# Shuffle reads issued later, more staging buffers, and another layout for the first batch, in a Fourier filter followed by a swish MLP

## The chip, the cores and the metric

The kernel runs on one core of one Trainium2 chip. The metric is the device time of one execution in microseconds (us). Most executions of one kernel agree within 0.3 to 0.5% in one round.

The engines are TensorE (PE; its weight loads are listed apart as PEld), VectorE (DVE), ScalarE (ACT), GpSimd (POOL) and SyncE (SP). SyncE does no arithmetic: it issues DMA transfers, in program order, and waits in that order too.

## The reference

A global filter along the sequence (rfft, product with a learned filter, irfft), then an MLP with the activation h * sigmoid(beta * h). Cut to what matters:

```python
# x: (8, 3008, 256); filt_r, filt_i: (1505, 256)
X = np.fft.rfft(x, axis=1)
y = np.fft.irfft(X * (filt_r + 1j * filt_i)[None], n=3008, axis=1)
# w_in: (256, 2048), w_out: (2048, 256), beta: (2048,)
h = y.reshape(8 * 3008, 256) @ w_in
out = (h / (1 + np.exp(-beta * h))) @ w_out
```

## The kernel before

The Fourier transform of length 3008 = 47 x 64 is done as two stages of matmuls with tables (stage 1 and stage 2), the product with the filter, and two inverse stages (3 and 4). Between the stages the data must change its place in the partitions.

For batch 0 this happens inside the core, in a **prologue**, with transposes on TensorE. For batches 1 to 7 it goes through DRAM. Each shuffle is a write of staging tiles and a read in another order: stage 1 writes d1, and a2 is read from it; stage 3 writes d2, and zz is read from it; stage 4 writes dy, and y is read from it by a transposing DMA.

The MLP is the **main loop** of 752 steps. A step handles 512 tokens and 128 hidden units: two matmuls into `hps`, a Silu on ScalarE into `gT`, and, two steps later, four matmuls into `acc`. Every 16 steps finish a block of 512 tokens. The filter work of the next batch is mixed in between the steps. A **window** is the stretch of steps that consume one batch: w0 has 80 steps, w1 to w7 have 96 each. In window w the stages 2 to 4 of batch w+1 and stage 1 of batch w+2 are placed; w0 also holds stage 1 of batch 1.

```python
apool = pool("apool", 3)          # staging tiles of stages 1 and 4, one tag
...
# prologue, batch 0: the inverse output of stage 3, one eviction per two frequencies
z_t = ypool.tile([P, NDC, J, KP], BF16, name="z_t", tag="y")      # J = 32, KP = 96
...
            evac(
                z_t[:, :, :, 4 * k0 : 4 * k0 + 8].rearrange("p c j a -> p c a j"),
                ps.rearrange("p c e (a j) -> p c (e a) j", j=J),
                True,                                              # on ScalarE
            )
...
def turn(g):                       # transposes: z_t is the stationary operand
    ...
                    nc.tensor.transpose(
                        pz[:KP, e, dc * P : (dc + 1) * P],
                        z_t[:, dc, JG * g + 4 * i + e, :],
                        ident[:],
                    )
...
def s1(b, i, on_act):              # a unit of stage 1, 16 units per batch
    ...
        s["a1"] = apool.tile([KP, JG, D], BF16, name="a1", tag="a1")   # each 4 units
    ...
    evac(s["a1"][:, jj : jj + 2, :], ps[:KP], on_act)
    if jj + 2 == JG:
        nc.sync.dma_start(s["d1r"][:, g * JG : (g + 1) * JG, :], s["a1"][:])
        if g == J // JG - 1:       # reads at once behind the last write
            ...
                nc.sync.dma_start(t[:], s["d1c"][:, h * KG : (h + 1) * KG, :])   # a2
            if b + 1 < B:
                xs[b + 1] = load_x(b + 1)
...
def place(w, lo, hi, units, clear=False):      # one unit per step at most
    a, z = first_step[w], first_step[w + 1]
    for n, go in enumerate(units):
        at = a + (z - a) * (lo + (hi - lo) * n / max(1, len(units) - 1))
        at = min(int(at), z - 1)
        if clear and (at % NFB < 2 or at % NFB > 13):
            at += (2 - at) % NFB
        while at in plan:
            at += 1
        plan[at] = go
...
    if w_ == 0:
        place(w_, 0.00, 0.15, u1(b, 0, n1, True))     # stage 1 of batch 1
        place(w_, 0.29, 0.62, u23(b), True)           # stages 2 and 3
        place(w_, 0.76, 0.87, u4(b))                  # stage 4
        if b + 1 < B:
            place(w_, 0.63, 0.75, u1(b + 1, 0, n1))   # stage 1 of the next batch
    else:
        place(w_, 0.03, 0.48, u23(b), True)
        place(w_, 0.64, 0.79, u4(b))
        if b + 1 < B:
            place(w_, 0.49, 0.63, u1(b + 1, 0, n1))
```

In `place`, stage 1 of the next batch comes last and moves past any taken step. Its 16 units do not fit in front of stage 4. In w0 the last eight of them (four of these only in w1), and in w1 to w5 the last three, therefore run behind stage 4.

## Time and profile before

The median was 901.64 us (901.03 to 905.14, four runs). The profiled execution took 894.5 us, which is at the fast end.

The page of the profile, first: busy time by engine, rows of busy tenths in 40 equal slices of the span of 892.4 us (PEclk is the granted TensorE clock in tenths), and two groups of instructions (line, engine, operation, shapes, count | busy us, mean ns | idle before).

```profile
PE 799.7 (90%) x5634; PEld 551.4 (62%) x5723; DVE 425.0 (48%) x656; ACT 617.0 (69%) x893; POOL 175.3 (20%) x189
...
PE   7449899559989999799978999799999999999997
...
PEclk9759999879989999999998999899999999999999
...
L662 ACT ACTIVATE gT<-hps,beta_sb 128x512 bf16<-128x512 f32 x752 | 516.5, 687 | 248.2 <-PE hps L653 226.9
...
L99 ACT ACTIVATE z_t<-psz 128x512 bf16<-128x512 f32 x12 | 31.2, 3023 | 4.6 <-PE psz L387 4.5
```

TensorE is busy 90% of the span. The clock row has holes: each digit below 9 is a slice in which TensorE ran partly at half speed. The two groups show the same shape, 128x512 float32 to bfloat16 on ScalarE. It takes 687 ns where the output is contiguous (gT) and 3023 ns where it is scattered (z_t).

The table of stretches (us from the span's start; busy us and count per engine; clock; DMA share; GB/s). The first two rows are the z_t evictions and the "turning" that follows them, up to the first Silu. The other rows are w0, w1 and w2.

```profile
core 0: us, PE busy (x) PEld busy (x) DVE busy (x) ACT busy (x) POOL busy (x), PEclk, DMA share, GB/s
31.60:65.80 34.20, 17.16 (x119) 11.81 (x119) 13.67 (x27) 34.10 (x14) 14.91 (x16) 0.60 0.43 76
65.80:77.10 11.30, 9.56 (x131) 8.32 (x132) 7.14 (x12) 5.36 (x14) 11.01 (x13) 0.87 0.32 94
77.10:179.60 102.50, 85.90 (x556) 56.87 (x566) 54.34 (x80) 64.07 (x101) 22.59 (x27) 0.94 0.61 151
179.60:296.50 116.90, 103.66 (x684) 69.11 (x694) 56.72 (x84) 71.56 (x108) 20.41 (x22) 0.92 0.49 124
296.50:400.40 103.90, 97.39 (x680) 67.27 (x689) 54.02 (x80) 71.70 (x108) 19.39 (x20) 0.98 0.52 139
```

In the first row ScalarE is busy 34.1 of 34.2 us: it is the limit there. In the other rows, compare the length with TensorE's busy time: 102.5 against 85.9 in w0, 117 against 103.7 in w1. The clock column is below 1.00 in all of them, so part of that busy time is itself stretched.

The waits (engine, line, what it waited for: us in total, times, longest):

```profile
PE hps L653 <- DMA y<-dy: 9.9, 2, 7.7
...
PE ps_2124 L516 <- DMA a_2093<-d_1676: 8.5, 1, 8.5
...
DVE a_2897 L101 <- DMA d_2716<-a_2719: 6.7, 1, 6.7
...
PE ps_2935 L567 <- DVE a_2897 L101: 4.1, 1, 4.1
```

And the chain of waits in w2 (start, duration, what), which shows how two of those lines hang together:

```profile
249.54 0.44 PE acc L680 x4
249.98 0.43 PE hps L653 x2
250.83 9.34 DMA d_2716<-a_2719
260.26 0.70 DVE a_2897 L101
...
261.59 0.85 PE acc L680 x4
```

The chain leaves TensorE at 250.4 us for the shuffle write of the oldest staging tile, which takes until 260.2 us. A stage-1 eviction (`a_2897`) needs a tile, all three are in use, and so it stands 6.7 us. TensorE itself works on until 256.9 us and then stands 4.1 us, because its next matmul waits for that eviction. From 261.0 us it goes on, at first with four acc matmuls in 0.85 us where they took 0.44 us before: half clock.

A last reading is worked out from the starts of the 752 Silu evictions in the trace. In w7, without filter work, eight steps take 7.0 us: that is the floor of TensorE.

| | first Silu at | w0 | w1 | w2 | w3 | w4 | w5 | w6 | w7 |
|---|---|---|---|---|---|---|---|---|---|
| before (us) | 77.1 | 102.5 | 117.0 | 103.9 | 105.3 | 104.9 | 99.8 | 92.5 | 83.0 |

### The profile page before, as it was taken

What the parts mean: (1) busy time and instruction counts of PE and PEld (TensorE: products, weight loads), DVE (VectorE), ACT (ScalarE), POOL (GpSimd) and SP (SyncE); (2) the same over time, 40 slices, a digit from 0 to 9 for tenths busy, and PEclk for the clock granted to TensorE, in tenths of its full rate; (3) what the DMA queues carried; (4) which work ended last, traced back from release to release, by engine and by line L of the source; (5) the groups of instructions that cost most, each with busy time, mean ns of one, the idle gap of its engine ahead of it and who ended that gap; (6) DMA issues with size and microseconds to landing.
All of it is one profiled execution on the core that took longest, in us unless ns stands there. A gap on an engine that the chain in (4) does not pass through costs nothing.

```text
span 892.4 us, 14629 instructions
## 1 busy us (share of the span) xinstructions
PE 799.7 (90%) x5634; PEld 551.4 (62%) x5723; DVE 425.0 (48%) x656; ACT 617.0 (69%) x893; POOL 175.3 (20%) x189
## 2 busy tenths in 40 slices
PE   7449899559989999799978999799999999999997
PEld 4336566337646776467655776467765676667665
DVE  7725485336544475427546265353656365421101
ACT  5797676328746787478854787467875788777775
POOL 4825251013200232003310132101310032000000
PEclk9759999879989999999998999899999999999999
DMA  8815627751186524674174821857135721551011
GB/s 168 170 38 112 171 77 208 159 145 60 55 222 134 166 86 110 182 169 132 59 176 136 210 73 47 217 120 192 60 96 188 198 67 61 171 129 48 24 49 48
DMA packets 132281, 110.06 MB, mean 123 GB/s; under 512 B 47010, under 2 KB 117683, under 8 KB 132211
## 3 DMA queue, kind: packets, MB, share of 16 engines
q1 hardware_dynamic: 127570, 95.74, 38.5%
q0 software_dynamic: 4640, 13.37, 8.9%
q8 instruction: 45, 0.74, 0.3%
q14 instruction: 26, 0.20, 0.1%
HBM read 54.01 MB, written 57.67 MB: 125 GB/s over the span
## 4 chain that ended last, share of the span: by engine, by line
PE 73%; DMA 12%; DVE 2%; issue 2%; SPq 2%; ACT 1%; POOL 0%; DVEq 0%; POOLq 0%; ACTq 0%
PE acc L680 33%; PE hps L653 30%; SPq L584 2%; DMA d_6478<-a_6481 1%; DMA d_3970<-a_3973 1%; DMA d_1676<-a_1679 1%; DMA d_5224<-a_5227 1%; DMA d_2716<-a_2719 1%; DMA y<-dy 1%; DMA d_7732<-a_7813 1%; DVE ost L692 1%; DVE yo L103 1%; DMA d_933<-a_1080 1%; DMA d_1676<-a_2040 1%; DMA d_5224<-a_5405 0%
## 5 line engine op out<-in xcount | busy, mean ns | idle before, releaser
L662 ACT ACTIVATE gT<-hps,beta_sb 128x512 bf16<-128x512 f32 x752 | 516.5, 687 | 248.2 <-PE hps L653 226.9
L680 PE MATMUL acc<-wout_sb,gT 128*128 128x256 bf16 x3008 | 461.1, 275 | 4.8 <-DVE ost L692 1.3
L653 PE MATMUL hps<-y,win_sb 128*128 128x512 bf16 (+7 forms) x1643 | 435.6, 354 | 10.2 <-DMA y<-dy 9.9
L680 PEld LDWEIGHTS <-gT 128*128 128x128 bf16 x3008 | 295.7, 99 | 187.7 <-issue 33.1
L653 PEld LDWEIGHTS <-win_sb 128*128 128x128 bf16 x1728 | 166.7, 99 | 34.9 <-issue 10.0
L534 POOL TENSOR_TENSOR v_t<-p_t,q_t 128x512 bf16<-128x512 f32 x84 | 106.5, 1268 | 305.9 <-DVE q_t L528 245.1
L692 DVE COPY ost<-acc 128x512 f32<-128x512 f32 x94 | 60.4, 684 | 200.8 <-PE acc L680 200.8
L113 POOL DMA_DIRECT2D xg<-in_x_dram x32 | 17.5, 546 | 238.2 <-PE ps_5651 L494 30.0
L516 PEld LDWEIGHTS <-t_102 128*128 128x128 bf16 x168 | 16.1, 98 | 29.7 <-issue 15.2
L99 ACT ACTIVATE z_t<-psz 128x512 bf16<-128x512 f32 x12 | 31.2, 3023 | 4.6 <-PE psz L387 4.5
L387 PE MATMUL psz<-t_103,pb_t 128*128 128x128 bf16 x48 | 10.1, 281 | 17.3 <-ACT z_t L99 10.7
L567 PEld LDWEIGHTS <-t_101 96*96 96x96 bf16 x112 | 14.3, 128 | 15.7 <-issue 2.1
L494 PEld LDWEIGHTS <-t_100 94*96 94x96 bf16 x112 | 13.9, 124 | 15.5 <-issue 2.8
L544 PEld LDWEIGHTS <-t_103 128*128 128x128 bf16 x168 | 16.0, 98 | 7.6 <-issue 2.3
L149 POOL TENSOR_SCALAR wout_sb<-ws,rbeta_sb 128x256 bf16<-128x256 f32 x16 | 14.5, 937 | 19.6 <-issue 19.3
L114 POOL DMA_DIRECT2D xg<-in_x_dram x32 | 16.4, 514 | 0.0
L184 PE MATMUL pw<-wz 128*128 128x512 bf16 x37 | 14.2, 470 | 1.2 <-DVE wz L178 1.2
L387 PEld LDWEIGHTS <-qb_t 128*128 128x128 bf16 x48 | 6.1, 129 | 11.6 <-issue 6.2
L138 POOL TENSOR_SCALAR fi_sb<-fi_sb 64x1536 f32<-64x1536 f32 x3 | 12.9, 4330 | 0.1
L387 PEld LDWEIGHTS <-pb_t 128*128 128x128 bf16 x48 | 6.3, 132 | 9.6 <-DVE pb_t L377 9.2
L387 PE MATMUL psz<-t3q,qb_t 128*128 128x128 bf16 x48 | 10.1, 286 | 0.5 <-DVE qb_t L378 0.5
L427 PE MATMUL pz<-ident,z_t 128*96 128x128 bf16 x64 | 5.4, 258 | 4.8 <-ACT z_t L99 4.8
(1037 smaller groups left out, 659.3 us busy)
## 6 DMA issues: line engine op xcount, KB each, us to landing
out_dram<-ost SPq DMA_DIRECT2D x47, 512.0 KB, 3.0
dy<-yo SPq DMA_DIRECT2D x28, 384.0 KB, 3.0
xg<-in_x_dram POOLq DMA_DIRECT2D x32, 320.0 KB, 6.0
ws<-in_moe_w_out_dram SPq DMA_DIRECT2D x4, 512.0 KB, 6.2
xg<-in_x_dram POOLq DMA_DIRECT2D x32, 56.0 KB, 6.0
fr_sb<-in_filt_r_dram SPq DMA_DIRECT2D x8, 192.0 KB, 6.3
fi_sb<-in_filt_i_dram SPq DMA_DIRECT2D x8, 192.0 KB, 7.2
d_934<-z SPq DMA_DIRECT2D x4, 384.0 KB, 2.8
```

The lines of the kernel that those rows point to most:

```text
L99: nc.scalar.activation(dst, src, ACT.Copy, scale=1.0 if scale is None else scale)
L113: nc.gpsimd.dma_start(t[:80], xv[:80, js, :])
L114: nc.gpsimd.dma_start(t[80:NP], xv[80:NP, js, :])
L387: nc.tensor.matmul(ps[:, dc, e, :], lhsT=src[:, e, dc * P : (dc + 1) * P], rhs=tab[:, k0 + e, :, :].rearrange("p c k -> p (c k)"), start=f ...
L516: nc.tensor.matmul(ps[:, e, :], lhsT=t2[:, k0 + e, :, :].rearrange("p c k -> p (c k)"), rhs=s["a2"][g][:, kk + e, :], start=True, stop=True,)
L534: nc.gpsimd.tensor_tensor(v_t[:], p_t[:], q_t[:], ALU.add)
L544: nc.tensor.matmul(ps[:, e, :], lhsT=t3[:, k0 + e, :, :].rearrange("p c k -> p (c k)"), rhs=v_t[:, e, :], start=True, stop=True,)
L584: nc.sync.dma_start_transpose(ys[b][:, c, :S], s["dy"][c, :S, :])
L653: nc.tensor.matmul(hps[:, pos - t0 : pos - t0 + ln], lhsT=win_sb[:, dc, fb * P : (fb + 1) * P], rhs=ys[b][:, dc, n0 : n0 + ln], start=(dc ...
L662: nc.scalar.activation(gT[:, :tn], hps[:, :tn], ACT.Silu, scale=beta_sb[:, fb : fb + 1])
L680: nc.tensor.matmul(acc[tb // 2][:, tb % 2, :], lhsT=gT[:, tb * P : (tb + 1) * P], rhs=wout_sb[:, fb, :], start=(fb == 0 and tb % 2 == 0), ...
L692: nc.vector.tensor_copy(ost[:, 2 * h : 2 * h + n, :], acc[h][:, :n, :])
```

## The change

Its intent: (a) issue the shuffle reads some steps after their writes, so that SyncE's in-order queue is not held up by them; (b) six staging tiles instead of three; (c) place stage 1 of the next batch ahead of stage 4, with two units per step in w0, every second one evicted by ScalarE; (d) in the prologue write z_t contiguously; (e) share the prologue's table work out differently: table evictions and fewer multiplies, the negated copies of the imaginary filter all on GpSimd, the beta constants computed earlier.

```diff
-    apool = pool("apool", 3)
+    apool = pool("apool", 6)
...
-            lo = AP(filt.tensor, filt.offset + k0 * D, [[N1 * D, H], [D, KG], [1, D]])
+            lo = AP(filt.tensor, filt.offset + k0 * D, [[N1 * D, H], [1, KG * D]])
...
+        ks_ = slice(8 * i, 8 * i + 8)
+        evac(t3[:, ks_, :, :].rearrange("p k c m -> p k (c m)"), pt[:], False)
+        for lo, to in ((M, 0), (0, M)):
+            evac(t3q[to : to + M, ks_, :, :]..., pt[lo : lo + M], True)
...
-    nc.vector.tensor_scalar_mul(fi_sb[:M, 0, :], fi_sb[:M, 0, :], keep[:M])
-    copy_imag(0, nc.vector)
-    copy_real(0)
-    nc.vector.tensor_scalar_mul(t3q[:, :, 0, :], t3[:, :, 1, :], nsg[:])
-    nc.vector.tensor_scalar_mul(t3q[:, :, 1, :], t3[:, :, 0, :], sg[:])
-    for g in range(1, NK // KG):
+    nc.gpsimd.tensor_scalar_mul(fi_sb[:M, 0, :], fi_sb[:M, 0, :], keep[:M])
+    for g in range(NK // KG):
         copy_imag(g, nc.gpsimd)
...
-    z_t = ypool.tile([P, NDC, J, KP], BF16, name="z_t", tag="y")
+    z_t = ypool.tile([P, NDC, KP, J], BF16, name="z_t", tag="y")
...
-                z_t[:, :, :, 4 * k0 : 4 * k0 + 8].rearrange("p c j a -> p c a j"),
-                ps.rearrange("p c e (a j) -> p c (e a) j", j=J),
+                z_t[:, :, 4 * k0 : 4 * k0 + 8, :].rearrange("p c (e a) j -> p c e (a j)", e=2),
+                ps[:],
...
-                        z_t[:, dc, JG * g + 4 * i + e, :],
+                        z_t[:, dc, :, JG * g + 4 * i + e],
...
     (the reads of a2, zz and y move out of s1, s23 and s4 into a2_read, zz_read, y_read)
...
         if w_ == 0:
-            place(w_, 0.00, 0.15, u1(b, 0, n1, True))
-            place(w_, 0.29, 0.62, u23(b), True)
-            place(w_, 0.76, 0.87, u4(b))
+            place(w_, 0.00, 0.14, u1(b, True))
+            place(w_, 0.19, 0.19, [lambda b=b: a2_read(b)], per=9)
+            place(w_, 0.28, 0.60, u23(b), True)
+            place(w_, 0.645, 0.645, [lambda b=b: zz_read(b)], per=9)
             if b + 1 < B:
-                place(w_, 0.63, 0.75, u1(b + 1, 0, n1))
+                place(w_, 0.61, 0.71, u1(b + 1, True), per=2)
+                place(w_, 0.78, 0.78, [lambda b=b: a2_read(b + 1)], per=9)
+            place(w_, 0.72, 0.81, u4(b, True), per=2)
+            place(w_, 0.85, 0.85, [lambda b=b: y_read(b)], per=9)
         else:
             place(w_, 0.03, 0.48, u23(b), True)
+            place(w_, 0.525, 0.525, [lambda b=b: zz_read(b)], per=9)
+            if b + 1 < B:
+                place(w_, 0.49, 0.63, u1(b + 1))
+                place(w_, 0.71, 0.71, [lambda b=b: a2_read(b + 1)], per=9)
             place(w_, 0.64, 0.79, u4(b))
-            if b + 1 < B:
-                place(w_, 0.49, 0.63, u1(b + 1, 0, n1))
+            place(w_, 0.84, 0.84, [lambda b=b: y_read(b)], per=9)
```

More of the change, by code (lines that the diff above doesn't have):

```diff
@@ L128, in load_filters @@
             )
-            nc.sync.dma_start(f_sb[:H, k0 : k0 + KG, :], lo)
+            nc.sync.dma_start(f_sb[:H, k0 : k0 + KG, :].rearrange("p k d -> p (k d)"), lo)
             nc.sync.dma_start(f_sb[H:M, k0 : k0 + KG, :], hi)
@@ L225 @@
     )
-    ip_f = small("ip_f")
-    nc.vector.tensor_copy(ip_f[:], ip[:])
-    nc.vector.tensor_scalar(ident[:], ic[:], ip_f[:], None, ALU.is_equal)
     m_p = bits("m_p", ip[:], ALU.bitwise_and, M - 1)
@@ L252 @@
     )
+    nc.vector.tensor_scalar(r[:], u[:], ROUND_C, ROUND_C, ALU.add, ALU.subtract)
+    nc.vector.tensor_tensor(u[:], u[:], r[:], ALU.subtract)
     def t2_part(part):
         if part == 0:
-            nc.vector.tensor_scalar(r[:], u[:], ROUND_C, ROUND_C, ALU.add, ALU.subtract)
+            nc.scalar.activation(t2[:, :, 0, :], u[:], ACT.Sin, scale=TWO_PI)
         elif part == 1:
-            nc.vector.tensor_tensor(u[:], u[:], r[:], ALU.subtract)
-            nc.scalar.activation(t2[:, :, 0, :], u[:], ACT.Sin, scale=TWO_PI)
-        elif part == 2:
             nc.scalar.activation(r[:], u[:], ACT.Abs)
@@ L270 @@
     gp = nc.gpsimd
-    hs, k2, keep, keep2, sg, nsg = (
-        small(n) for n in ("hs", "k2", "keep", "keep2", "sg", "nsg")
-    )
+    ip_f = small("ip_f")
+    gp.tensor_copy(ip_f[:], ip[:])
+    gp.tensor_scalar(ident[:], ic[:], ip_f[:], None, ALU.is_equal)
+    hs, k2, keep, keep2 = (small(n) for n in ("hs", "k2", "keep", "keep2"))
     gp.tensor_scalar(hs[:], m_p[:], float(H), None, ALU.is_ge)
@@ L281 @@
     gp.tensor_scalar(keep[:], keep[:], 1.0, None, ALU.add)
-    gp.tensor_scalar(sg[:], hs[:], -2.0, 1.0, ALU.mult, ALU.add)
-    gp.tensor_scalar(nsg[:], c_p[:], 2.0, -1.0, ALU.mult, ALU.add)
-    gp.tensor_tensor(nsg[:], nsg[:], sg[:], ALU.mult)
-    gp.tensor_scalar(sg[:], nsg[:], -1.0, None, ALU.mult)
     nc.gpsimd.memset(t4[:], 0.0)
@@ L304 @@
                 ps[:, :, :KP].rearrange("p j k -> p k j"),
-                dc == 1,
+                i < 4 or (i < 6 and dc == 1),
             )
         warm(2)
-        if i % 2 == 1:
-            t2_part(i // 2)
+        if i >= 3 and i < 6:
+            t2_part(i - 3)
     a2s = []
@@ L324 @@
                 )
-        evac(a2s[-1][:, 3 * (i % 2) : 3 * (i % 2) + 3, :], pb[:], i % 2 == 1)
+        evac(a2s[-1][:, 3 * (i % 2) : 3 * (i % 2) + 3, :], pb[:], False)
+    bps = opsum.tile([P, NFB], F32, name="bps", tag="acc")
+    id_f = setup.tile([NFB, NFB], F32, name="id_f", tag="id_f")
+    nc.vector.tensor_copy(id_f[:], ident[:NFB, :NFB])
+    nc.tensor.transpose(bps[:], bt[:], id_f[:])
+    tiny = setup.tile([P, NFB], F32, name="tiny", tag="tiny")
+    nc.vector.tensor_copy(beta_sb[:], bps[:])
+    nc.vector.tensor_tensor(tiny[:], beta_sb[:], beta_sb[:], ALU.mult)
+    nc.vector.tensor_scalar(tiny[:], tiny[:], 1e-12, None, ALU.is_lt)
+    nc.vector.scalar_tensor_tensor(beta_sb[:], tiny[:], 2e-6, beta_sb[:], ALU.mult, ALU.add)
+    nc.vector.reciprocal(rbeta_sb[:], beta_sb[:])
+    copy_real(0)
     for i in range(3):
@@ L333 @@
             )
-        evac(t3[:, 8 * i : 8 * i + 8, :, :].rearrange("p k c m -> p k (c m)"), pt[:], i != 0)
+        ks_ = slice(8 * i, 8 * i + 8)
+        evac(t3[:, ks_, :, :].rearrange("p k c m -> p k (c m)"), pt[:], False)
+        for lo, to in ((M, 0), (0, M)):
+            evac(
+                t3q[to : to + M, ks_, :, :].rearrange("p k c m -> p k (c m)"),
+                pt[lo : lo + M],
+                True,
+            )
     tp = opsum.tile([KP, NP], BF16, name="tp", tag="acc")
@@ L399 @@
         warm(1)
-    bps = opsum.tile([P, NFB], F32, name="bps", tag="acc")
-    id_f = setup.tile([NFB, NFB], F32, name="id_f", tag="id_f")
-    nc.vector.tensor_copy(id_f[:], ident[:NFB, :NFB])
-    nc.tensor.transpose(bps[:], bt[:], id_f[:])
-    tiny = setup.tile([P, NFB], F32, name="tiny", tag="tiny")
-    nc.vector.tensor_copy(beta_sb[:], bps[:])
-    nc.vector.tensor_tensor(tiny[:], beta_sb[:], beta_sb[:], ALU.mult)
-    nc.vector.tensor_scalar(tiny[:], tiny[:], 1e-12, None, ALU.is_lt)
-    nc.vector.scalar_tensor_tensor(beta_sb[:], tiny[:], 2e-6, beta_sb[:], ALU.mult, ALU.add)
-    nc.vector.reciprocal(rbeta_sb[:], beta_sb[:])
     sp.close()
@@ L499, in s1, with a2_read @@
             nc.sync.dma_start(s["d1r"][:, g * JG : (g + 1) * JG, :], s["a1"][:])
-            if g == J // JG - 1:
-                s["a2"] = []
-                for h in range(NK // KG):
-                    t = a2pool.tile([P, KG, D], BF16, name="a2", tag="a2")
-                    nc.sync.dma_start(t[:], s["d1c"][:, h * KG : (h + 1) * KG, :])
-                    s["a2"].append(t)
-                if b + 1 < B:
-                    xs[b + 1] = load_x(b + 1)
+            if g == J // JG - 1 and b + 1 < B:
+                xs[b + 1] = load_x(b + 1)
+    def a2_read(b):
+        s = st[b]
+        s["a2"] = []
+        for h in range(NK // KG):
+            t = a2pool.tile([P, KG, D], BF16, name="a2", tag="a2")
+            nc.sync.dma_start(t[:], s["d1c"][:, h * KG : (h + 1) * KG, :])
+            s["a2"].append(t)
     def s23(b, i):
@@ L553, in s23, with zz_read, s4 @@
                 nc.sync.dma_start(s["d2c"][:, g * KG : (g + 1) * KG, :], s["z"][:])
-                if g == NK // KG - 1:
-                    s["zz"] = []
-                    for h in range(J // JG):
-                        t = zzpool.tile([KP, JG, D], BF16, name="zz", tag="zz")
-                        nc.sync.dma_start(t[:], s["d2r"][:, h * JG : (h + 1) * JG, :])
-                        s["zz"].append(t)
-    def s4(b, i):
+    def zz_read(b):
+        s = st[b]
+        s["zz"] = []
+        for h in range(J // JG):
+            t = zzpool.tile([KP, JG, D], BF16, name="zz", tag="zz")
+            nc.sync.dma_start(t[:], s["d2r"][:, h * JG : (h + 1) * JG, :])
+            s["zz"].append(t)
+    def s4(b, i, on_act):
         s = st[b]
@@ L572, in s4 @@
             ps[:KP].rearrange("p (j c d) -> p c j d", j=2, c=NDC),
-            False,
+            on_act,
             inv_scale,
@@ L580, in s4, with y_read @@
             )
-            if g == J // JG - 1:
-                ys[b] = ypool.tile([P, NDC, NK * P], BF16, name="y", tag="y")
-                for c in range(NDC):
-                    nc.sync.dma_start_transpose(ys[b][:, c, :S], s["dy"][c, :S, :])
-                del st[b]
+    def y_read(b):
+        s = st.pop(b)
+        ys[b] = ypool.tile([P, NDC, NK * P], BF16, name="y", tag="y")
+        for c in range(NDC):
+            nc.sync.dma_start_transpose(ys[b][:, c, :S], s["dy"][c, :S, :])
     NBLK = (TOK + TB - 1) // TB
@@ L594, with place, u1 @@
     plan = {}
-    def place(w, lo, hi, units, clear=False):
+    def place(w, lo, hi, units, clear=False, per=1):
         a, z = first_step[w], first_step[w + 1]
+        last_at = a
         for n, go in enumerate(units):
             at = a + (z - a) * (lo + (hi - lo) * n / max(1, len(units) - 1))
-            at = min(int(at), z - 1)
+            at = max(min(int(at), z - 1), last_at)
             if clear and (at % NFB < 2 or at % NFB > 13):
                 at += (2 - at) % NFB
-            while at in plan:
+            while len(plan.get(at, ())) >= per:
                 at += 1
-            plan[at] = go
-    def u1(b, lo, hi, act=False):
+            plan.setdefault(at, []).append(go)
+            last_at = at
+    def u1(b, act=False):
         def unit(i):
@@ L615, in unit, with u4 @@
             return go
-        return [unit(i) for i in range(lo, hi)]
+        return [unit(i) for i in range(J // 2)]
     def u23(b):
         return [lambda i=i: s23(b, i) for i in range(NK // 2 + VLAG)]
-    def u4(b):
-        return [lambda i=i: s4(b, i) for i in range(J // 2)]
+    def u4(b, act=False):
+        return [lambda i=i: s4(b, i, act and i % 2 == 1) for i in range(J // 2)]
     for w_ in range(B - 1):
         b = w_ + 1
-        n1 = J // 2
         if w_ == 0:
-            place(w_, 0.00, 0.15, u1(b, 0, n1, True))
-            place(w_, 0.29, 0.62, u23(b), True)
-            place(w_, 0.76, 0.87, u4(b))
+            place(w_, 0.00, 0.14, u1(b, True))
+            place(w_, 0.19, 0.19, [lambda b=b: a2_read(b)], per=9)
+            place(w_, 0.28, 0.60, u23(b), True)
+            place(w_, 0.645, 0.645, [lambda b=b: zz_read(b)], per=9)
             if b + 1 < B:
-                place(w_, 0.63, 0.75, u1(b + 1, 0, n1))
+                place(w_, 0.61, 0.71, u1(b + 1, True), per=2)
+                place(w_, 0.78, 0.78, [lambda b=b: a2_read(b + 1)], per=9)
+            place(w_, 0.72, 0.81, u4(b, True), per=2)
+            place(w_, 0.85, 0.85, [lambda b=b: y_read(b)], per=9)
         else:
             place(w_, 0.03, 0.48, u23(b), True)
+            place(w_, 0.525, 0.525, [lambda b=b: zz_read(b)], per=9)
+            if b + 1 < B:
+                place(w_, 0.49, 0.63, u1(b + 1))
+                place(w_, 0.71, 0.71, [lambda b=b: a2_read(b + 1)], per=9)
             place(w_, 0.64, 0.79, u4(b))
-            if b + 1 < B:
-                place(w_, 0.49, 0.63, u1(b + 1, 0, n1))
+            place(w_, 0.84, 0.84, [lambda b=b: y_read(b)], per=9)
     blk = {}
@@ L666 @@
         if s in plan:
-            plan[s]()
+            for go in plan[s]:
+                go()
         if s >= LAG:
```

## The prediction

> **What bounds it now** (table of stretches; starts of the 752 Silu evictions). A prologue: first Silu at 77.1 us. The main loop, 752 steps: in the last 96, free of filter work, eight steps take 7.0 us, TensorE at full clock. With a batch of filter work mixed in, 96 steps need about 96 us (92.5 were taken by window 6, which lacks only 16 stage-1 matmuls of 0.21 us). The windows took: w0 (80 steps) 102.5, w1 117.0, w2 to w4 103.9, 105.3, 104.9, w5 99.8, w6 92.5, w7 83: 16 us in w0, 21 in w1, 4 to 9 in each of w2 to w5 are TensorE stalls, some 66 us together. Then a tail of 6 us.
>
> **The stalls** (waits, chain of waits, DMA issues). In w2 to w4 a stage-1 eviction waits 7 to 10 us for the shuffle write of an earlier staging tile (three buffers; the write queues behind four zz reads and lands after 9 to 11 us instead of 3 to 6). TensorE idles 4 to 6 us in stage 4, then runs 3.4 to 6.8 us at half clock. In w0 the transposing y reads land 8 to 10 us late. In w1 the a2 reads are 8.5 us late: the last stage-1 units were pushed behind stage 4. The Trainium skill, "TensorE: Matmul & The Clock Gate", section "HAM oscillation", says that waits over about 3.4 us bring the half clock; this trace's clock agrees.
>
> **The prologue.** From 31.6 to 65.8 us ScalarE limits: twelve z_t evictions 2.6 us apart (3.02 us each, elements scattered 192 bytes apart). The same shape written contiguously took 0.69 us (gT).
>
> **What the change does.**
> - z_t: 12 x (2.6 - 0.6) = 24 us off ScalarE. GpSimd limits next, with all four negated filter copies (4.1 to 4.3 us each) after the t4 scaling: about 26 + 1.3 + 0.8 + 4 x 4.2 + 1.6 = 46 us, then three pairs of products (1.2 us each): z_t ends near 51, not 66. The turning transposes now load weights at a 64-byte stride; the skill's "SBUF — State Buffer" (cachelines note) warns of that, no trace here prices it; I allow 1 us. First Silu near 62: **-15 us**.
> - VectorE loses a 4.5 us t3q multiply, ScalarE gains six table evictions of 1 us: even.
> - Six staging buffers, stage 1 wholly before stage 4: w2 to w4 near 97 each, **-23**; w5 **-3**.
> - w1, a2 read early: near 97, **-20**.
> - w0: stage 4 ends at step 66 of 80, not 75; y follows some 14 us later, near step 80; 0 to 3 us of stall may stay: **-14**.
> - Contiguous filter loads, early beta: under 1.
>
> No matmul gets shorter. Sum -75 of 902: **827 us**, 8 in 10 within **812 to 848**. Faster by over 2%: 0.97; within 2%: 0.02; slower: 0.01.
>
> **What would show it.** First Silu at 58 to 66 us; z_t evictions near 0.7 us; late products waiting for GpSimd's fi copies; w1 to w5 at 95 to 99 us, eight steps at most 9; no half clock after 75 us except perhaps at the end of w0; no stage-1 eviction waiting on a shuffle write; matmul count unchanged, TensorE busy above 94%.
>
> **What would make it wrong.** Strided weight loads at 0.1 to 0.2 us more each (64: +6 to 13 us). The y read, issued at step 80 of 96 beside the last stage-4 unit, needing 14 us: each window boundary could stall 1 to 4 us and drop the clock. x loads, now earlier, colliding with a2 reads and yo writes. ScalarE, with doubled units in w0, delaying Silu.

## More of the kernel before

The instructions on the tile z_t (durations in ns as min/median/max, first and last start):

```profile
L427 PEld LDWEIGHTS <-z_t x64: 123/123/203, 65.9 to 73.2; 128*96 128x96 bf16 x64
...
L99 ACT ACTIVATE z_t<-psz x12: 2727/3121/3122, 31.6 to 62.7; 128x512 bf16<-128x512 f32 x12
```

## The result

The changed kernel took 845.59 us in the median (842.92 to 846.41, four runs) against 901.64. The ratio is 0.9366, 95% interval 0.9334 to 0.9398. Ratios here are the mean time of one kernel's fast runs over that of the other's of the same rounds, so they are not quite the ratios of the medians quoted. The time lies within the stated range, 19 us above the stated value.

| | first Silu at | w0 | w1 | w2 | w3 | w4 | w5 | w6 | w7 |
|---|---|---|---|---|---|---|---|---|---|
| before (us) | 77.1 | 102.5 | 117.0 | 103.9 | 105.3 | 104.9 | 99.8 | 92.5 | 83.0 |
| after (us) | 67.6 | 110.5 | 98.9 | 96.3 | 96.3 | 96.3 | 96.3 | 92.5 | 83.0 |
| difference | -9.5 | +8.0 | -18.1 | -7.6 | -9.0 | -8.6 | -3.5 | 0 | 0 |

The differences add up to -48.3 us, which is the difference of the two profiled spans (892.4 and 844.1). The medians differ by 56 us, because the profiled execution of before was 7 us faster than its median.

So w1 to w5 gained as foreseen, the prologue gained less, and w0 became longer. The page after, in the lines that answer to those of before:

```profile
PE 797.0 (94%) x5634; PEld 553.8 (66%) x5723; DVE 410.9 (49%) x638; ACT 602.0 (71%) x911; POOL 179.9 (21%) x189
...
PE   7589886979999999999999999999999999999997
...
PEclk9778998889999999999999999999999999999999
...
L674 ACT ACTIVATE gT<-hps,beta_sb 128x512 bf16<-128x512 f32 x752 | 516.1, 687 | 193.4 <-PE hps L665 171.4
...
L99 ACT ACTIVATE z_t<-psz 128x512 bf16<-128x512 f32 x12 | 7.1, 597 | 8.8 <-PE psz L395 8.7
```

TensorE is busy 94% of a span of 844.1 us. The clock row is now 9 from the tenth slice (190 us) on. The z_t evictions take 597 ns instead of 3023. The same stretches as before (z_t evictions, turning, w0, w1, w2):

```profile
32.70:49.10 16.40, 13.01 (x118) 8.86 (x118) 12.56 (x21) 9.98 (x14) 16.29 (x14) 0.88 0.56 92
49.10:67.60 18.50, 17.49 (x131) 16.21 (x132) 7.41 (x12) 5.31 (x12) 14.28 (x16) 0.63 0.51 118
67.60:178.20 110.60, 90.87 (x562) 58.76 (x571) 46.29 (x68) 72.10 (x117) 23.51 (x28) 0.92 0.66 161
178.20:277.10 98.90, 98.19 (x680) 66.90 (x690) 54.20 (x80) 71.50 (x108) 19.31 (x20) 0.97 0.52 143
277.10:373.40 96.30, 95.59 (x680) 66.70 (x689) 54.19 (x80) 71.71 (x109) 19.32 (x20) 1.00 0.53 147
```

The z_t stretch fell from 34.2 to 16.4 us, and GpSimd, busy 16.29 us of it, is now its limit. The turning grew from 11.3 to 18.5 us with the same 131 matmuls. In w2 TensorE is busy 95.6 of 96.3 us at full clock: no wait is left to be removed there. The instructions on z_t:

```profile
L424 PEld LDWEIGHTS <-z_t x64: 238/257/269, 49.1 to 62.8; 128*96 128x96 bf16 x64
...
L99 ACT ACTIVATE z_t<-psz x12: 592/597/597, 32.7 to 48.5; 128x512 bf16<-128x512 f32 x12
```

The weight loads of the turning went from a median of 123 ns to 257. The waits:

```profile
PE ps_1800 L570 <- DMA zz<-d_932: 7.7, 1, 7.7
...
DVE qb_t L386 <- POOL fi_sb L138: 6.1, 2, 5.0
...
PE hps L665 <- DMA y<-dy: 4.6, 2, 2.6
...
PE ps_1208 L517 <- DMA a_1131<-d_931: 3.8, 1, 3.8
```

The wait for a staging tile is gone. A wait of 7.7 us for zz in w0 is new. SyncE's queue in w0 (start, time, issue) shows how late zz is:

```profile
131.47 0.32 SPq L496 DMA_DIRECT2D d_1615<-a_1618  x1
132.52 0.36 SPq L554 DMA_DIRECT2D d_932<-z  x1
139.61 2.43 SPq L561 DMA_DIRECT2D zz<-d_932  x4
```

And in the kernel before:

```profile
140.33 1.73 SPq L558 DMA_DIRECT2D zz<-d_934  x4
```

The reads of zz wait 7 us for the last write of d2, which stands right behind a stage-1 write of batch 2. They are issued 72.0 us after the start of w0 (139.6 - 67.6). Before it was 63.2 us (140.3 - 77.1). Yet stage 4 was moved ahead, from step 60 to step 58, while the last unit of stage 3 stands at step 51 in both kernels.

The 8.8 us have two parts. The last write of d2 is issued 4.6 us later in the window (64.9 us after its start against 60.3), since the steps before it took longer. And it takes 7.1 us until SyncE can go on, where it took 2.9 us before. Then the first read of zz takes 8.0 us to land instead of 3.7. Beside these transfers (130 to 140 us) SyncE and GpSimd issued a stage-1 write, an output write and eight loads of x; in the kernel before there was only an output write.

### The profile page after: what moved, and what is told of

The parts are those of the page before. It is cut to its first block, busy times and chain, and to the rows that moved or that the text cites. A ratio compares the mean times of both kernels' runs of the same rounds, so it can differ in the third digit from the quotient of the medians.

```text
span 844.1 us, 14640 instructions
## 1 busy us (share of the span) xinstructions
PE 797.0 (94%) x5634; PEld 553.8 (66%) x5723; DVE 410.9 (49%) x638; ACT 602.0 (71%) x911; POOL 179.9 (21%) x189
## 2 busy tenths in 40 slices
DMA packets 132280, 110.06 MB, mean 130 GB/s; under 512 B 47009, under 2 KB 117682, under 8 KB 132210
## 4 chain that ended last, share of the span: by engine, by line
PE 85%; DMA 7%; issue 3%; DVE 2%; POOL 2%; SPq 1%; ACT 1%; DVEq 0%; POOLq 0%; ACTq 0%
PE acc L693 38%; PE hps L665 35%; DMA fi_sb<-in_filt_i_dram 2%; PE pz L424 1%; DVE ost L705 1%; POOL fi_sb L138 1%; DMA zz<-d_932 1%; DMA xg<-in_x_dram 1%; DMA dy<-yo 1%; DMA y<-dy 1%; DMA d_931<-a_1078 1%; DMA a_3015<-d_2714 1%; DMA a_6777<-d_6476 0%; DMA a_1131<-d_931 0%; DVE q_t L529 0%
## 5 line engine op out<-in xcount | busy, mean ns | idle before, releaser
L114 POOL DMA_DIRECT2D xg<-in_x_dram x32 | 16.4, 513 | 0.0
L138 POOL TENSOR_SCALAR fi_sb<-fi_sb 64x1536 f32<-64x1536 f32 x4 | 16.3, 4100 | 0.1
L395 PE MATMUL psz<-t3q,qb_t 128*128 128x128 bf16 x48 | 7.9, 244 | 8.3 <-DVE qb_t L386 7.7
L99 ACT ACTIVATE z_t<-psz 128x512 bf16<-128x512 f32 x12 | 7.1, 597 | 8.8 <-PE psz L395 8.7
L424 PE MATMUL pz<-ident,z_t 128*96 128x128 bf16 x64 | 11.2, 353 | 0.5 <-ACT z_t L99 0.5
L424 PEld LDWEIGHTS <-z_t 128*96 128x96 bf16 x64 | 10.8, 257 | 0.8 <-ACT z_t L99 0.8
L101 DVE COPY zz<-pz 96x1024 bf16<-96x1024 bf16 x8 | 5.5, 687 | 9.8 <-PE pz L424 9.8
```

Of the source, the lines that this page charges most:

```text
L114: nc.gpsimd.dma_start(t[80:NP], xv[80:NP, js, :])
L138: eng.tensor_scalar_mul(fi_sb[M:P, ks_, :], fi_sb[:M, ks_, :], -1.0)
L424: nc.tensor.transpose(pz[:KP, e, dc * P : (dc + 1) * P], z_t[:, dc, :, JG * g + 4 * i + e], ident[:],)
```

## The experiments

Twelve kernels ran; each gave correct results. Each was timed beside the kernel before on its own chip; the median of before was 898 to 902 us in the four groups (runs 1 to 4, 5 to 8, 9 and 10, 11 and 12; one chip each). Runs of different groups are best compared by their ratios. The table of windows gives the first Silu and the windows in us, worked out as above from each trace; w6 (92.5) and w7 (83.0) were the same in all.

| run | median | ratio to before | first Silu | w0 | w1 | w2 | w3 | w4 | w5 |
|---|---|---|---|---|---|---|---|---|---|
| after | 845.59 | 0.9366 | 67.6 | 110.5 | 98.9 | 96.3 | 96.3 | 96.3 | 96.3 |
| 1 z_t scattered again | 853.97 | 0.9469 | 78.5 | 107.1 | 98.8 | 96.3 | 96.3 | 96.3 | 96.2 |
| 2 z_t in runs | 834.23 | 0.9248 | 58.7 | 106.9 | 97.9 | 96.3 | 96.6 | 96.3 | 96.2 |
| 3 three buffers | 881.42 | 0.9773 | 68.2 | 114.0 | 105.2 | 103.5 | 104.6 | 105.2 | 98.2 |
| 4 first window earlier | 830.98 | 0.9219 | 67.3 | 97.2 | 97.6 | 96.3 | 96.3 | 96.3 | 96.3 |
| 5 reads at once | 842.90 | 0.9376 | 67.4 | 108.7 | 97.9 | 96.3 | 96.3 | 96.3 | 96.3 |
| 6 before, six buffers | 861.81 | 0.9579 | 77.6 | 101.3 | 111.5 | 96.5 | 98.1 | 97.0 | 97.1 |
| 7 runs 2 and 4 together | 825.44 | 0.9176 | 59.4 | 98.7 | 97.8 | 96.3 | 96.3 | 96.3 | 96.3 |
| 8 first copy on VectorE | 820.46 | 0.9125 | 54.6 | 98.6 | 97.9 | 96.3 | 96.3 | 96.3 | 96.3 |
| 9 x load later | 819.73 | 0.9103 | 54.5 | 97.8 | 97.6 | 96.3 | 96.3 | 96.3 | 96.3 |
| 10 a2 read before stage 4 | 822.30 | 0.9134 | 54.5 | 100.5 | 97.7 | 96.3 | 96.3 | 96.3 | 96.3 |
| 11 x load spread | 816.95 | 0.9049 | 54.5 | 95.0 | 97.9 | 96.3 | 96.3 | 96.3 | 96.3 |
| 12 a2 read after y | 810.74 | 0.8982 | 54.5 | 91.0 | 96.3 | 96.3 | 96.3 | 96.3 | 96.3 |

### 1. z_t scattered again

```diff
-    z_t = ypool.tile([P, NDC, KP, J], BF16, name="z_t", tag="y")
+    z_t = ypool.tile([P, NDC, J, KP], BF16, name="z_t", tag="y")
...   (eviction and transposes as in the kernel before)
```

> The changed kernel with the first batch's inverse output z_t laid out and evicted as before (single elements 192 bytes apart). Theory (the new layout trades ScalarE time for strided weight loads): z_t evictions return to about 3.0 us each and the twelve of them end 15 to 18 us later (about 65 instead of 49 us), but the turning stretch from the last of them to the first Silu shrinks from 18.5 to about 11 us, with weight loads back from 257 to about 156 ns; first Silu at 75 to 78 us, total +8 to +11 us (853 to 857). Rival (the turning stretch is long for another cause, such as GpSimd or DMA work that now falls beside it): the turning stretch stays above 15 us and the total grows by 15 us or more.

Measured: 853.97 us, 8 us more than the changed kernel. The evictions are back at 3023 ns in the mean. The last of them starts at 63.5 us, and the first Silu is at 78.5 us. The weight loads are back at a median of 140 ns, and the turning from the first transpose (66.7 us) takes 11.8 us. So the layout alone is worth about 11 us at the first Silu: 17 us gained by the evictions and 7 us given back in the turning. The rival, another cause for the long turning, falls.

### 2. z_t in runs of 16 bytes

The old layout, but the eviction follows the order of the destination. PSUM is then read with strides instead, and eight bfloat16 elements are written side by side.

```diff
-                z_t[:, :, 4 * k0 : 4 * k0 + 8, :].rearrange("p c (e a) j -> p c e (a j)", e=2),
-                ps[:],
+                z_t[:, :, :, 4 * k0 : 4 * k0 + 8],
+                ps.rearrange("p c e m -> p c (e m)").rearrange("p c (a j) -> p c j a", j=J),
...   (z_t as [P, NDC, J, KP] and the transposes as in the kernel before)
```

> The changed kernel with the old layout of z_t, but the eviction walks it in the order of the destination, so that eight elements (16 bytes) are written side by side and PSUM is read strided. Theory (scattered two-byte writes made the old eviction slow, strided weights make the new turning slow): evictions at 0.6 to 0.8 us, weight loads at about 156 ns, turning stretch about 11 us, first Silu near 60 us, total -6 to -9 us (837 to 840). Rival (strided PSUM reads cost as much as scattered writes): evictions at 1.5 us or more and no gain.

Measured: 834.23 us, better than expected. The instructions on z_t in this run, and its turning as a row of the table of stretches:

```profile
L424 PEld LDWEIGHTS <-z_t x64: 119/123/125, 48.8 to 54.8; 128*96 128x96 bf16 x64
...
L99 ACT ACTIVATE z_t<-psz x12: 591/597/598, 32.3 to 48.1; 128x512 bf16<-128x512 f32 x12
```

```profile
48.80:58.70 9.90, 8.24 (x131) 6.99 (x133) 6.96 (x12) 5.34 (x13) 7.66 (x9) 1.00 0.91 201
```

Both sides are had: evictions at 597 ns as in the contiguous layout, weight loads at 123 ns as in the old one. The turning takes 9.9 us at full clock. The scattered writes, not the layout, made the old eviction slow; strided reads of PSUM cost nothing here.

This run also prices the strided weight load. The first thirty-two transposes took 2.03 us here at full clock, 63 ns each. In the changed kernel they took 5.51 us, 172 ns each, beginning at full clock too: the clock fell only in the course of the turning, as two more rows of its table of stretches show.

```profile
49.00:53.00 4.00, 3.88 (x24) 3.88 (x24) 1.37 (x2) 0.07 (x1) 4.00 (x5) 1.00 1.07 212
53.00:57.00 4.00, 3.68 (x32) 3.55 (x31) 1.83 (x3) 1.34 (x3) 3.17 (x4) 0.59 0.82 208
```

64 x (172 - 63) ns = 7.0 us, of the 8.6 us by which the turning is longer than here (18.5 against 9.9). That it grew by nearly the same 7.0 us, namely 7.2, from before to after is luck: the kernel before began its turning at half clock too, 27 transposes 107 ns apart instead of 56, which is 1.4 us by estimate. The half clock came on top, from the second of these rows on, although TensorE is recorded as busy all the time. It cost the transposes little (sixteen took 2.83 us, 177 ns each), it may account for the other 1.6 us of the turning, which was not measured apart, and it cost 1.5 us in the first eight steps of w0 (9.5 against 8.0 us). Why the clock fell is not shown. It is not that transposes alone cannot bring the full clock: in the kernel before TensorE stood from 61.0 to 65.9 us, then ran transposes alone, and at 68.7 us these went from 107 to 56 ns apart. In the changed kernel they start 165 ns apart; that this left the array idle between them is an argument only.

### 3. Three buffers

```diff
-    apool = pool("apool", 6)
+    apool = pool("apool", 3)
```

> The changed kernel with three staging buffers instead of six. Theory (the buffers remove the mid-window stall of w2 to w5): a stage-1 eviction again waits for the shuffle write of an earlier tile, w2 to w5 go from 96.3 to 101 to 105 us each, total +20 to +40 us. Rival (placing stage 1 wholly ahead of stage 4 and the reads behind the writes removed the stall, the buffers hardly matter): w2 to w5 stay below 98 us, total within 6 us of the changed kernel.

Measured: 881.42 us, +36 us. The waits of this run:

```profile
DVE a L101 <- DMA d<-a: 37.6, 5, 8.7
...
PE ps L491 <- DVE a L101: 24.8, 6, 6.0
```

The wait of stage-1 evictions for shuffle writes is back, and TensorE's 6 us waits with it. w2 to w4 are at 103.5 to 105.2 us, as in the kernel before. The rival, that placement removed this stall, falls: without the buffers the new placement is no better in w2 to w4 than the old.

### 4. First window earlier

```diff
-            place(w_, 0.00, 0.14, u1(b, True))
-            place(w_, 0.19, 0.19, [lambda b=b: a2_read(b)], per=9)
-            place(w_, 0.28, 0.60, u23(b), True)
-            place(w_, 0.645, 0.645, [lambda b=b: zz_read(b)], per=9)
+            place(w_, 0.00, 0.09, u1(b, True), per=2)
+            place(w_, 0.12, 0.12, [lambda b=b: a2_read(b)], per=9)
+            place(w_, 0.23, 0.53, u23(b), True)
+            place(w_, 0.56, 0.56, [lambda b=b: zz_read(b)], per=9)
             if b + 1 < B:
-                place(w_, 0.61, 0.71, u1(b + 1, True), per=2)
+                place(w_, 0.57, 0.67, u1(b + 1, True), per=2)
```

> The changed kernel with the first window's stages 1 to 3 of batch 1 placed earlier (stage 1 two units per step, stages 2 and 3 over 0.23 to 0.53 of the window, zz read at 0.56, stage 1 of batch 2 at 0.57 to 0.67); stage 4 unchanged. Theory (w0 is bound by the latency of the chain of shuffles; stage 4 was placed before its zz data could land): the 7.7 us wait for zz falls below 2 us, the half-clock stretch after it goes, w0 falls from 110.5 to 93 to 98 us, total -12 to -17 us (829 to 833). Rival (w0 is bound by engines or DMA volume, doubled units crowd ScalarE and VectorE): w0 stays above 104 us.

Measured: 830.98 us, and w0 at 97.2. All that TensorE still waits for a DMA in the main loop:

```profile
PE hps L665 <- DMA y<-dy: 3.8, 2, 2.4
...
PE ps L517 <- DMA a<-d: 2.0, 1, 2.0
```

The wait for zz is gone. w0 was bound by the latency of its chain of shuffles, not by engines or by the amount of data in all: the same units, more crowded than before, fit into 13 us less. The run does two things at once, though: the front of the chain starts earlier, and the zz reads (issued at 123.8 us) now go ahead of the stage-1 writes and x loads of the next batches (from 125.5 us on). How much each gave is not shown.

### 5. Reads at once

Every read goes back behind its last write; buffers and placement stay.

```diff
+            if g == J // JG - 1:
+                a2_read(b)
+                if b + 1 < B:
+                    xs[b + 1] = load_x(b + 1)
...   (zz_read and y_read likewise; the seven placed reads are taken out)
```

> The changed kernel with every shuffle read issued directly behind its last write again, buffers and placement kept. Theory (the delay of the reads is worth little once there are six buffers and stage 1 is wholly ahead of stage 4): w2 to w5 within 1 us of 96.3 each; in w0 the a2 reads of batch 2 now go ahead of the yo writes, so y comes 2 to 5 us later; total +0 to +6 us. Rival (the delay itself removed the stalls of w2 to w5): these windows go back above 99 us each, total +12 us or more.

Measured: 842.90 us, ratio 0.9376 (0.9348 to 0.9404) against 0.9366 for the changed kernel: no difference that the runs could show. w2 to w5 are 96.3 us each. The delay of the reads, the first item of the change, is worth nothing once there are six buffers. A detail of the expectation missed: y did not come later. TensorE's wait for it fell from 4.6 to 2.4 us. In this run stage 4 itself was held 8.3 us by zz.

### 6. The kernel before with six buffers

```diff
-    apool = pool("apool", 3)
+    apool = pool("apool", 6)
```

> The kernel before with six staging buffers and nothing else changed. Theory (the buffers alone cure w2 to w4, the placement cures w1): w2 to w5 at 96 to 98 us each instead of 104, w1 still above 108 us because the last four stage-1 units of batch 2 stay behind stage 4, w0 little changed; total -22 to -32 us (870 to 880). Rival (buffers and placement are both needed): w2 to w4 stay above 101 us.

Measured: 861.81 us, ratio 0.9579. The gain is 37 us in the medians, more than expected; the profiled spans (892.4 and 861.1) differ by 31. The spread accounts for the rest: the profiled execution of before (894.5) lies 3.8 us below the median of this group (898.35), that of run 6 (863.17) 1.4 us above its own. w2 to w5 are at 96.5 to 98.1 us. w1 is still 111.5 us, with its wait for a2:

```profile
PE ps L516 <- DMA a<-d: 14.7, 5, 8.9
```

The line holds five waits, the longest 8.9 us. So one line of the change, the buffers, makes 7.4 + 7.2 + 7.9 + 2.7 = 25.2 us of the 28.7 us gained in w2 to w5. What it leaves undone in w1 the placement repairs: with it, in run 3, the wait of w1 for a2 is gone even without the buffers, and what remains there is the staging wait.

### 7. Runs 2 and 4 together

> The changed kernel with both repairs: z_t in the old layout written in runs of 16 bytes, and the first window's stages 1 to 3 earlier. Theory (the two losses lie in different stretches and add up): first Silu near 58.7 us and w0 near 95 us; 845.6 - 11.4 - 14.6 = 820 us, between 817 and 823. Rival (with an earlier start of w0 the loads of x and weights or the chain of shuffles becomes late again): above 826.

Measured: 825.44 us, where 817 to 823 was expected. The two repairs do not quite add up. w0 is 98.7 us and not 95: TensorE waits 3.8 us for the a2 reads of batch 1, against 2.0 in run 4, and its third group of eight steps takes 13.8 us instead of 11.0. With a quicker turning and quicker steps, less time passes for the same chain of transfers. The rival was right in kind.

### 8. First copy on VectorE

```diff
-    nc.gpsimd.tensor_scalar_mul(fi_sb[:M, 0, :], fi_sb[:M, 0, :], keep[:M])
-    for g in range(NK // KG):
+    nc.vector.tensor_scalar_mul(fi_sb[:M, 0, :], fi_sb[:M, 0, :], keep[:M])
+    copy_imag(0, nc.vector)
+    for g in range(1, NK // KG):
```

> As the run with both repairs, and the scaling and negated copy of the first filter group back on VectorE, as in the kernel before (0.33 and 0.95 us there against 0.93 and 4.1 us on GpSimd). Theory (GpSimd's chain of copies is what the product loop waits for, 5.0 us at its start and 1.1 us at the last group): first q product at 27 instead of 31 us, last z_t eviction 3 to 5 us earlier, first Silu at 54 to 56 us, total -3 to -5 us against that run. Rival (TensorE at half clock paces the loop): the start moves but the end of the loop moves by less than 1.5 us.

Measured: 820.46 us, first Silu at 54.6 instead of 59.4 us. The first q product starts at 26.8 us instead of 31.0 in the changed kernel. Within the change, moving that copy to GpSimd therefore cost some 5 us.

### 9. x load later

The load of x for batch 2 is issued at step 24 of w0.

```diff
-            if g == J // JG - 1 and b + 1 < B:
+            if g == J // JG - 1 and b + 1 < B and b != 1:
...
+            place(w_, 0.30, 0.30, [lambda b=b: xs.update({b + 1: load_x(b + 1)})], per=9)
```

> As the run with the first copy on VectorE, with the load of x for batch 2 issued at step 24 of the first window, no longer right behind stage 1 of batch 1. Theory (that load, 41% of the DMA engines' time between 60 and 82 us, slows the last shuffle writes of batch 1, which land 7.9 us after the wait begins, so that TensorE waits 3.0 us for a2 and runs at half clock): the writes land within 5.5 us, the a2 wait falls below 1 us, steps 16 to 24 take 9 to 10 us instead of 13.2, total -3 to -5 us (815 to 818). Rival (the writes land late because of their own volume): the wait stays above 2 us, total within 1.5 us of that run.

Measured: 819.73 us, no gain in the sum that the runs could show (ratio 0.9103 against 0.9125 in run 8, with overlapping intervals). Yet the mechanism was right. The a2 reads are issued at 67.1 us instead of 74.1, TensorE's wait for a2 is gone, and steps 16 to 24 take 9.2 us instead of 13.2. A new wait took the gain back. TensorE's instructions after a wait, in this run (the wait in brackets):

```profile
79.05 0.38 PE L546 MATMUL ps<-v_t,t 128*128 128x256 bf16 x2 [0.66 <-POOL v_t L536]
...
88.78 0.38 PE L546 MATMUL ps<-v_t,t 128*128 128x256 bf16 x2 [3.05 <-POOL v_t L536]
```

The eight DMA issues take 4.2 us of GpSimd, from 83.3 to 87.4 us, and the sum `v_t` queues behind them. TensorE waits 3.05 us, falls to half clock, and steps 24 to 32 take 13.1 us.

### 10. a2 read before stage 4

As run 9, with this:

```diff
-                place(w_, 0.78, 0.78, [lambda b=b: a2_read(b + 1)], per=9)
+                place(w_, 0.69, 0.69, [lambda b=b: a2_read(b + 1)], per=9)
```

> As the run with the late x load, with the a2 reads of batch 2 issued ahead of stage 4's writes in the first window (0.69 instead of 0.78). Theory (these 1.5 MB of reads stand between the yo writes in the queue and make y late by some 3 us): the wait for y at the end of w0 falls from 3.3 us to below 1.5 us, steps 72 to 80 take 8 to 9 us instead of 10.5, total -1 to -3 us against the run with the late x load. Rival (the y chain is bound by its own writes and transposes): no change beyond 0.7 us.

Measured: 822.30 us, and wrong in sign: the wait for y grew from 3.3 to 6.2 us. SyncE waits in order. It stood until 133.1 us for the stage-1 writes to land before it could issue the a2 reads, and the stage-4 writes behind them came out from 135.5 us on, instead of from 128.6 us.

### 11. x load spread

As run 9, but one tile of x at a time, between the sums of GpSimd.

```diff
-            place(w_, 0.30, 0.30, [lambda b=b: xs.update({b + 1: load_x(b + 1)})], per=9)
+            xs[b + 1] = []
+            for g_, f_ in enumerate((0.24, 0.27, 0.305, 0.33)):
+                place(w_, f_, f_, [lambda b=b, g=g_: xs[b + 1].extend(load_x(b + 1, (g,)))], per=9)
```

> As the run with the late x load, but the four tiles of x are issued one by one between the sums of stage 2 on GpSimd. Theory (the late load in one piece held GpSimd for 4.2 us ahead of a sum, TensorE waited 3.1 us for it and fell to half clock, steps 24 to 32 took 13.1 us): no wait above 1.5 us for GpSimd's sums, steps 24 to 32 at 8 to 9 us, steps 16 to 24 stay near 9.2, w0 at 92.5 to 94.5 us, total -3 to -5 us against that run (814.5 to 817). Rival (any issue of x between the sums costs TensorE): w0 stays above 96 us.

Measured: 816.95 us (four runs). Steps 16 to 24 take 9.5 us, steps 24 to 32 take 8.4, w0 95.0. The longest wait for GpSimd's sums is 1.3 us. Part of the gain went to the end of the window: the wait for y is 5.0 us, as the same chain now has less time.

### 12. a2 read after y

As run 11, with the a2 reads of batch 2 behind the y reads:

```diff
-                place(w_, 0.78, 0.78, [lambda b=b: a2_read(b + 1)], per=9)
             place(w_, 0.72, 0.81, u4(b, True), per=2)
             place(w_, 0.85, 0.85, [lambda b=b: y_read(b)], per=9)
+            if b + 1 < B:
+                place(w_, 0.87, 0.87, [lambda b=b: a2_read(b + 1)], per=9)
```

> As the run with the spread x load, with the a2 reads of batch 2 issued behind the y reads of the first window instead of between stage 4's writes. Theory (reads ahead of y in the one queue make y late; ahead of stage 4's writes they cost 2.9 us in another run): the y wait of 3.3 us at the end of w0 falls below 1.5 us, steps 72 to 80 take 8 to 9.5 us, total -1 to -3 us. Rival (the a2 reads then come too late for step 82): a new wait for a2 of 2 us or more at the start of w1, total unchanged or worse.

Measured: 810.74 us (810.55 to 811.21, five runs), ratio 0.8982 (0.8952 to 0.9013), the fastest of all: 4% below the changed kernel by the two ratios (0.8982 / 0.9366 = 0.959). SyncE's queue at the end of w0 and the page:

```profile
124.05 8.14 SPq L581 DMA_DIRECT2D dy<-yo  x4
...
135.25 6.32 SPq L590 DMA_TRANSPOSE y<-dy  x2
141.61 3.79 SPq L508 DMA_DIRECT2D a<-d  x4
```

```profile
PE 783.7 (97%) x5723; PEld 541.3 (67%) x5723; DVE 411.2 (51%) x640; ACT 602.7 (75%) x911; POOL 176.1 (22%) x187
...
PEclk9899999999999999999999999999999999999999
```

The transposing reads are issued at 135.3 us instead of 139.8, the wait for y is 1.4 us, and w0 is 91.0 and w1 96.3 us. The a2 reads, issued at 141.6 us, are in time: no wait for a2 is left. The gain of 6 us is more than the 1 to 3 expected, since the half clock at the start of w1 went as well (w1 fell from 97.9 to 96.3 us).

## Why the prediction was right or wrong

The time lies in the range, 2.4 us below its upper edge, but two of the five parts of the sum were far off (the prologue and w0), and luck helped. By the profiles the sum misses by 26.7 us. The medians miss by 19 us only because the profiled execution of before, from which the stalls were read, was 7 us faster than its median.

- **The mechanism of w2 to w5 was right, and so was the size**: -23 and -3 us predicted, -25.2 and -3.5 measured. Run 3 shows that the buffers are necessary, run 6 that they are nearly enough there (25.2 of 28.7 us).
- **w1 was right**: -20 predicted, -18.1 measured. Run 6, with the old placement, keeps the late a2 reads and gains 5.5 us in w1; run 3, with the new placement and three buffers, loses them and gains 11.8. So the placement is the larger cause and the buffers a smaller one.
- **The prologue was half right**: -15 predicted, -9.5 measured. The z_t evictions ended at 49.1 us (near 51 predicted) with GpSimd as the new limit, as foreseen and as run 8 shows. The step that failed is "I allow 1 us" for the weight loads at a 64-byte stride. They cost 7.0 us, 109 ns on each of 64 transposes, and a half clock came with them. The prediction's last paragraph held this possibility (0.1 to 0.2 us each), and it should have stood in the sum.
- **w0 was wrong in sign**: -14 predicted, +8.0 measured. The step that failed is "stage 4 ends at step 66 of 80, not 75; y follows some 14 us later". It carried stage 4 forward without asking whether zz, two transfers earlier in the same chain, could be there. It was not: zz was issued 8.8 us later in the window than before, landed more slowly, and stage 4 stood 7.7 us. The prediction's last paragraph feared the earlier x loads, but beside a2 and yo and not beside zz. Run 4 moves the front of the chain instead and takes 13.3 us off w0 in the profile.
- **The account closes**: the misses are +5.5 us in the prologue, +22 in w0, +1.9 in w1, -2.2 in w2 to w4 and -0.5 in w5, together 26.7, the distance between the sum of -75 and the -48.3 of the profiles.
- **Feared and not seen**: the y read at step 80 of w1 to w5 cost nothing; w2 to w5 are 96.3 us each. "No half clock after 75 us except perhaps at the end of w0" was wrong: the waits for a2 and zz brought it in the middle of w0 too (clock 0.92 in the row of w0).
- **Without effect**: the delayed reads (run 5, with six buffers), and the contiguous filter loads. The page counts 132281 DMA packets before and 132280 after: the two access patterns name the same run of memory.
- The Trainium skill, "TensorE: Matmul & The Clock Gate", section "What's actually happening", gives about 3.4 us of idle time for the fall to half clock. This agrees roughly: in the changed kernel's trace the waits of 3.8 us (a2), of 7.7 us (zz) and the two of 2.1 and 2.6 us close together (y) were each followed by half clock, and so were those of 3.05 us in run 9 and of 2.6 us (a2 in w0) in the kernel before; the waits of 2.0 us (a2) in run 4 and of 1.3 us for a sum were not.

Still open: why the granted clock fell in the turning of the changed kernel; how the 13.3 us of run 4 divide between an earlier chain and less crowded transfers; and what the table evictions and the earlier beta constants of the change were worth, since no run takes them out (the z_t evictions began at 32.7 us, 1.1 us later than before).

## What to carry to other kernels

When a chain of transfers is moved forward, check each link against the arrival of its data: in w0, stage 4 was due before zz had landed, and the window grew by 8 us. In an in-order issue queue the place of a wait matters more than the transfer behind it, so put what is needed last behind what is needed first (run 12 against run 11). And when an eviction is slow for scattered writes, try the order of the destination, with strided reads of PSUM, before changing a layout that the next stage reads.

## What the Trainium skill lacked or had wrong

- "SBUF — State Buffer", the cachelines note, says that accesses that cross to a new 16-byte line pay, and gives no size for TensorE's weights. Here 96 columns 64 bytes apart took 257 ns per load against 123 ns side by side (medians), and a transpose 172 ns against 63 ns.
- The same note calls any non-contiguous PSUM access slow for matmuls and says nothing of evictions. ScalarE's eviction was not slowed: 597 ns with PSUM read in strides (run 2), 597 ns with PSUM read in order. Single bfloat16 elements written 192 bytes apart took 3121 ns in the median; runs of eight cost nothing extra. No page prices this.
- "GPSIMD Engine Reference", section "Engine selection", calls one-input work on GpSimd roughly line-rate. Here the negated copy of 64x1536 float32 took 4.1 us on GpSimd and 0.955 us on VectorE.
- "TensorE: Matmul & The Clock Gate" ties the half clock to idle time, and its Part 4 says that the full clock does not engage for transposes. In the kernel before it did, at 68.7 us, with nothing but transposes since 65.9 us. In the turning of the changed kernel the clock fell to half between 53 and 57 us, while TensorE was recorded as busy 3.88 us (49 to 53 us) and 3.68 us (53 to 57 us).
- No page says how long an issue on GpSimd holds up its arithmetic: here eight issues of x loads held it 4.2 us, 0.52 us each (run 9).
